# Normalising and turning the second chunk of tokens earlier, by transfers instead of through TensorE

## The chip, the cores and the metric

The kernel runs on one core of a Trainium2 chip. The metric is the device time in microseconds of one execution of the whole program. The core's engines are named as the profile names them: PE (TensorE, matmuls; PEld its weight loads), DVE (VectorE), ACT (ScalarE), POOL (GpSimd) and SP (SyncE, which here only issues transfers). PSUM is the memory that PE writes its products into; SBUF is the working memory of all engines.

## The reference

A sequence of 2048 tokens with 640 features goes through one layernorm, and then through attention with 32 heads of 20 features and through an MLP with its own layernorm and 1536 hidden features. Their results are added to the input.

```python
def _A_ref(x, wqkv, wo):                       # 32 heads, Dh = 20
    qkv = (x @ wqkv).reshape(B, S, 3, H, Dh) ...
    scores = einsum("bhqd,bhkd->bhqk", q, k) * (Dh ** -0.5)
    o = einsum("bhqk,bhkd->bhqd", softmax(scores), v)
    return o.reshape(B, S, D) @ wo
def _B_ref(x, w1, b1, w2, b2):
    h = gelu(_layernorm(x) @ w1 + b1)
    return h @ w2 + b2
x  = A_x                                       # 1 x 2048 x 640, float32
xn = _layernorm(x)
return x + _A_ref(xn, A_wqkv, A_wo) + _B_ref(xn, B_w1, B_b1, B_w2, B_b2)
```

## The kernel before

All matmuls take 16-bit operands in two parts, a high and a low one: `a*b` is computed as high*high + high*low + low*high (the three entries of `PASS`). So each operand is first scaled to a power of two, then copied to float16 on ACT (the high part), and the rest is subtracted on DVE (the low part).

The program has a first part, up to about 227 us, that normalises the tokens and makes Q, K and V, and a long second part in which attention and the MLP run interleaved. The change is in the first part. There the order of each engine's instructions is the order in which the code issues them (`manual_schedule`); nothing is reordered by a planner. An engine does its instructions in that order and waits at the first whose data is not there. SP issues its transfers in the same way. Each transfer of SP's queue also counts on one of eight semaphores in turn, and waits for the transfer eight places ahead of it.

The tokens come in four chunks of 512, loaded as four rows of 128 tokens (`xts[c][j]`, `load_x`). For each chunk c:

- `norm_a(c)` takes mean and variance of the rows on DVE and a power on POOL; `norm_b(c)` makes the row factor exact, normalises the four rows in place (L258) and starts the second layernorm's factor (`norm_b2`, again with a power on POOL); `norm_c(c)` ends that factor on DVE and POOL sends it to DRAM (`rscr`, L274: 512 values of 4 bytes), from where the MLP reads it much later.
- The chunk is turned, so that features lie on the partitions: `xnts[c]`, in a high and a low part. Before, this happens in two ways. The first and second chunk go through PE: `transp` issues 128x128 transposes against an identity into PSUM, `transp_out` evicts them as the high part (ACT) and the low part (DVE). The third and fourth chunk go by `turn(c, j)`: ACT and DVE split row j into its high and low part in a `row` buffer (three of these), and a transposing transfer on SP puts it into `xnts[c]`. In both ways a copy of the finished `xnts[c]` goes to DRAM (`xscr`) for the MLP.
- Five steps tt of `qk(c, tt)` make Q and K of the chunk: each is 30 matmuls into a PSUM buffer of the pool `psS` (three buffers, tag "s"), emptied by `qk_out` (L340 on ACT, L341 on DVE), which also sends both parts to DRAM (`qkscr`). Four calls of `vproj(c, j)` make V from the same turned chunk, emptied by `vproj_out` (L408 on ACT, L410 on DVE).

Into this are fitted the preparations of the weights. In the first chunk: `sums`, `scale_of` and `split_qkv` for K and V (V in the fourth step, tt = 3: L431 on ACT, L432 on DVE); `ask(n)`, which has SP issue the next n loads of w2 (six blocks, L500) and w1 (five blocks, L503); and `some(n)`, the next n slices of squares and splits of w2, w1 and wo, which wait for those loads on ACT.

Before the change, the second chunk's statistics are taken in the third step of the first chunk (tt = 2). `norm_b(1)` comes behind the first V product, `norm_c(1)` behind the second. The transposes of the second chunk stand behind the second and the third V product, in PE's queue between the V products. The second chunk's copy to `xscr` is issued when the last part is evicted; three of the five w1 blocks stand ahead of it in SP's queue, two behind it, and then the third chunk's rows (`load_x(2)`).

Of the kernel before, what the change touches and what calls it, by code (L numbers as in the profile page):

```python
# [18 lines left out]
P = 128  # L19
S, D, H, DH, F = 2048, 640, 32, 20, 1536  # L20
KD = D // P
# [23 lines left out]
def mha_mlp_kernel(tc, x, wqkv, wo, w1, b1, w2, b2, out):  # L45
    nc = tc.nc
# [3 lines left out]
    with (  # L50
# [10 lines left out]
        xscr = dram.tile([P, KD, 2, S], F16, name="xscr")  # L61
# [17 lines left out]
        ident = keep.tile([P, P], F32, name="ident")  # L79
# [84 lines left out]
        with tc.tile_pool(name="pa", bufs=2) as pa, tc.tile_pool(name="pa1", bufs=1) as pa1, tc.manual_schedule():  # L164
# [7 lines left out]
            xts = {}  # L172
# [98 lines left out]
            def norm_c(c):  # L271
                mv, ve, r, r2 = rs.pop(c)
                newton(r2, ve, "b")
                nc.gpsimd.dma_start(rscr[c * 512 : (c + 1) * 512].rearrange("(j p) -> p j", p=P), r2)  # L274

            xnts = {}

            def transp(c, k0, pts):
                if k0 == 0:
                    xnts[c] = pa.tile([P, KD, 2, 512], F16, tag="xnt", name=f"xnt{c}")  # L280
                if k0 + 2 > KD:
                    pt = psM.tile([P, 512], F32, tag="m", name="pt4")[:, None, :]
                else:
                    pt = psS.tile([P, 2, 512], F32, tag="s", name="pt")
                for j in range(4):
                    for k in range(min(2, KD - k0)):
                        nc.tensor.transpose(pt[:, k, j * P : (j + 1) * P],
                                            xts[c][j][:, (k0 + k) * P : (k0 + k + 1) * P], ident)
                pts.append((c, k0, pt))

            def transp_out(c, k0, pt):
                nk = min(2, KD - k0)
                ks = slice(k0, k0 + nk)
                nc.scalar.activation(xnts[c][:, ks, 0, :], pt[:, :nk], AF.Copy)
                nc.vector.tensor_sub(xnts[c][:, ks, 1, :], pt[:, :nk], xnts[c][:, ks, 0, :])
                if k0 + 2 > KD:
                    nc.sync.dma_start(xscr[:, :, :, c * 512 : (c + 1) * 512], xnts[c])
                    del xts[c]

            def turn(c, j):  # L300

                if j == 0:
                    xnts[c] = pa.tile([P, KD, 2, 512], F16, tag="xnt", name=f"xnt{c}")
                xv = xts[c][j].rearrange("p (k n) -> p k n", k=KD)
                row = pa.tile([P, KD, 2, P], F16, tag="row", name="row", bufs=3)
                nc.scalar.activation(row[:, :, 0, :], xv, AF.Copy)
                nc.vector.tensor_sub(row[:, :, 1, :], xv, row[:, :, 0, :])
                nc.sync.dma_start(xnts[c].rearrange("p k s t -> p (k s) t")[:, :, j * P : (j + 1) * P],
                                  row.rearrange("p k s n -> p (k s n)"), transpose=True)
                if j == 3:  # L310
                    nc.sync.dma_start(xscr[:, :, :, c * 512 : (c + 1) * 512], xnts[c])
                    del xts[c]
# [104 lines left out]
            def sums(tag, ws):  # L417
                accs[tag] = squares(ws, junk)

            def scale_of(tag):  # L420
                pw[tag] = pow2(accs[tag], tag)
                scales[tag] = keep.tile([P, 1], F32, name=f"s_{tag}")
                nc.vector.tensor_scalar(scales[tag], pw[tag][1], 4096.0, None, ALU.mult)
                if tag in "qk":
                    q = "qk".index(tag)
                    nc.vector.tensor_scalar(qks[:, q : q + 1], pw[tag][0], QKTOP, 2.0**-22, ALU.min, ALU.mult)

            def split_qkv(n, ks=range(KD), c0=0, c1=D):
                q = "qkv".index(n)
                for k in ks:  # L430
                    nc.scalar.activation(wv[:, k, q, 0, c0:c1], stage[n][:, k, c0:c1], AF.Copy, scale=scales[n])  # L431
                    nc.vector.scalar_tensor_tensor(wv[:, k, q, 1, c0:c1], stage[n][:, k, c0:c1], scales[n],  # L432
                                                   wv[:, k, q, 0, c0:c1], ALU.mult, ALU.subtract)
# [75 lines left out]
            def ask(n):  # L509
                for _ in range(n):  # L510
                    next(asked, None)
# [21 lines left out]
            pts = [psS.tile([P, 2, 512], F32, tag="s", name="pt") for _ in range(2)]  # L533
            pt = [pts[0][:, 0], pts[0][:, 1], pts[1][:, 0], pts[1][:, 1]]
# [17 lines left out]
            for c in range(4):  # L552
                nxt = c + 1 if c < 3 else None
                for tt in range(5):
                    if c == 0 and tt == 1:
                        norm_b2(0)
                        norm_c(0)

                        nc.scalar.activation(junk[:, :1], ones[:, :1], AF.Exp)
                        ps = qk(0, 1, lambda: scale_of("k"))  # L560
                        hl = qk_out(0, 0, first)
                        split_qkv("q", c0=4 * P)
                        split_qkv("k")
                    else:
                        ps = qk(c, tt)
                    if tt == 3:
                        lengths(4)

                    if c == 0:
                        if tt == 0:  # L570
                            split_qkv("q", c0=2 * P, c1=4 * P)
                            sums("k", [stage["k"][:, 0:3], stage["k"][:, 3:]])
                            first = ps
                            continue
                        elif tt == 1:
                            qk_sq(0, 0, hl)
                        elif tt == 2:
                            sums("v", [stage["v"][:, 0:3], stage["v"][:, 3:]])
                            norm_a(1)
                        elif tt == 3:  # L580
                            scale_of("v")
                            split_qkv("v")
                    else:

                        step = tt - (c == 1)
                        if nxt and 0 <= step < 3:
                            (norm_a, norm_b, norm_c)[step](nxt)
                            some(1)
                        else:
                            some(2)  # L590
                    qk_out(c, tt, ps)

                    ask((0, 1, 2, 2, 1)[tt] if c == 0 else 0)
                    if nxt and c > 0 and tt >= 2:
                        for j in ((0,), (1, 2), (3,))[tt - 2]:
                            turn(nxt, j)
                    if c == 3 and tt == 2:
                        early = [load_features(mc) for mc in range(2)]
                if c == 1:
                    load_x(3)  # L600
                if c == 3:
                    stack = load_stack(0, 0)
                    for _ in range(6):
                        next(stack)
                for j in range(4):
                    ps = vproj(c, j)
                    if j == (0 if c == 3 else 1):
                        lengths(10)
                    if c == 0:
                        if j < 2:  # L610
                            (norm_b, norm_c)[j](1)

                        pts = []
                        for k in ((), (0,), (2, 4), ())[j]:
                            transp(1, k, pts)
                        for t in pts:
                            transp_out(*t)
                    if j == 0 and c == 3:
                        shifts()
                        for _ in stack:  # L620
                            pass
                    some(2 if c < 3 else 1)
                    vproj_out(c, j, ps)
# [660 lines left out]
```

## Time and profile before

| | |
|---|---|
| median of 3 runs | 1341.68 us (1340.11 to 1343.48) |
| profiled execution, its own time | 1341.9 us |
| its span, first to last instruction | 1340.0 us |
| mean granted clock of PE | 0.999 |
| busy: PE, ACT, DVE | 1328.6, 1130.1, 1055.9 us |
| first chunk's Q, K and V on PE | from 15.3 us |
| second chunk's first Q and K product on PE | 68.5 us |
| third chunk's | 119.6 us |
| fourth chunk's | 169.6 us |

In a timeline row the first number is the start from the beginning of the span, the second the time from the start of the first to the end of the last instruction in the row, then engine, line, operation, what is written and read, and xN for N instructions; in brackets the idle time of the engine ahead of it and what ended it. In a row of the waits the three numbers are the total, the number of times and the longest. In a row of a table by windows there are, behind the window and its length, the busy time and the count of PE, weight loads, DVE, ACT and POOL, then the granted clock of PE, the share of the 16 transfer engines and the GB/s moved. SPq and POOLq are transfers issued by SP and POOL; a row of the transfers has their count, their size and the median time from issue to landing.

### The profile page before, as it was taken

How to read it: one execution, taken by the hardware profiler on the slowest of the kernel's cores; microseconds unless marked ns; L12 is line 12 of the kernel's file. 1: busy time of each engine (PE TensorE's matmuls, PEld its weight loads, DVE VectorE, ACT ScalarE, POOL GpSimd, SP SyncE). 2: the span in 40 equal slices, each digit the busy share in tenths (PEclk: the TensorE clock that was granted, in tenths of full speed). 3: DMA queues.
4: the chain of work that ended last, by engine and by line, in shares of the span. 5: the costliest groups of instructions: out<-in, count | busy, mean ns of one | idle time of the engine just before them, and what ended most of it. 6: DMA issues, size and time to landing. Idle time of an engine off the chain costs nothing.

```text
span 1340.0 us, 29065 instructions
## 1 busy us (share of the span) xinstructions
PE 1328.6 (99%) x11647; PEld 588.6 (44%) x11647; DVE 1055.9 (79%) x1436; ACT 1130.1 (84%) x1306; POOL 37.5 (3%) x85
## 2 busy tenths in 40 slices
PE   9999999999999999999999999999999999999998
PEld 6645546443344433434433344334333444333366
DVE  7766945998779887978897878888887988888732
ACT  7754525999999999999999999999999999999900
POOL 3010000000000000000000000000000000000000
PEclk9999999999999999999999999999999999999999
DMA  9768731111112232122322032313032323334366
GB/s 279 253 197 183 125 128 58 34 53 43 49 52 78 87 83 73 44 69 67 91 76 71 19 103 56 88 56 94 19 83 78 85 64 103 90 113 121 104 208 187
DMA packets 100150, 129.54 MB, mean 97 GB/s; under 512 B 24276, under 2 KB 66328, under 8 KB 100012
## 3 DMA queue, kind: packets, MB, share of 16 engines
q1 hardware_dynamic: 96652, 120.25, 31.5%
q0 software_dynamic: 2912, 6.90, 2.8%
q8 instruction: 92, 1.51, 0.5%
q10 hardware_dynamic: 448, 0.51, 0.1%
q14 instruction: 46, 0.38, 0.1%
HBM read 82.14 MB, written 42.51 MB: 93 GB/s over the span
## 4 chain that ended last, share of the span: by engine, by line
PE 86%; DVE 6%; ACT 4%; issue 2%; DMA 1%; SPq 0%; ACTq 0%; DVEq 0%; POOL 0%; POOLq 0%
PE o L742 28%; PE s L711 18%; PE py L1006 13%; PE pu L976 10%; PE qkp L325 7%; PE z L1089 4%; PE vp L398 3%; DVE low L725 2%; ACT p L713 1%; PE warm L222 1%; ACT wv L431 1%; DMA oa<-opart 0%; DVE u L914 0%; ACT qkhl L340 0%; DVE u L916 0%
## 5 line engine op out<-in xcount | busy, mean ns | idle before, releaser
L713 ACT ACTIVATE p<-s 128x1024 f32<-128x1024 f32 x1024 | 972.8, 1045 | 35.0 <-PE s L711 28.6
L725 DVE TENSOR_TENSOR low<-p 128x1024 f16<-128x1024 f32 x512 | 614.5, 1219 | 144.9 <-ACT p L713 144.2
L742 PE MATMUL o<-p,vfull 128*32 128x512 bf16 (+1 forms) x4096 | 430.0, 493 | 0.0
L711 PE MATMUL s<-qs,ks 61*128 61x512 f16 x2048 | 311.9, 381 | 1.1 <-ACT p L713 1.1
L711 PEld LDWEIGHTS <-ks 61*128 61x128 f16 x2048 | 61.1, 94 | 280.1 <-issue 279.1
L1006 PE MATMUL py<-w2t,hT 128*128 128x320 f16 x1152 | 178.5, 300 | 0.5 <-DVE u L914 0.3
L976 PE MATMUL pu<-xm,w1t 128*128 128x256 f16 x1440 | 178.2, 273 | 0.0
L976 PEld LDWEIGHTS <-w1t 128*128 128x128 f16 x1440 | 131.0, 98 | 64.6 <-issue 51.0
L1006 PEld LDWEIGHTS <-hT 128*128 128x128 f16 x1152 | 102.5, 98 | 88.5 <-issue 54.1
L325 PE MATMUL qkp<-xnt,wv 128*128 128x512 f16 x600 | 131.1, 379 | 1.4 <-DVE vfull L410 0.9
L742 PEld LDWEIGHTS <-vfull 128*32 128x32 f16 x3072 | 59.8, 95 | 139.2 <-issue 108.5
L742 PE MATMUL o<-low,vfull 128*32 128x512 f16 x1024 | 102.9, 378 | 0.4 <-DVE low L725 0.2
L325 PEld LDWEIGHTS <-wv 128*128 128x128 f16 x600 | 58.1, 98 | 71.4 <-DVE vfull L410 1.2
L742 PEld LDWEIGHTS o<-p,vfull 128*32 128x32 f32 x2048 | 62.5, 108 | 52.6
L1089 PE MATMUL z<-w1t,ot 128*128 128x320 f16 x480 | 69.0, 304 | 0.4 <-DVE acc L1047 0.4
L340 ACT ACTIVATE qkhl<-qkp,qks 128x1024 f16<-128x1024 f32 (+1 forms) x24 | 23.2, 967 | 54.6 <-PE qkp L325 33.0
L398 PE MATMUL vp<-wv,xnt 128*128 128x320 f16 x480 | 66.7, 299 | 0.0
L1089 PEld LDWEIGHTS <-ot 128*128 128x128 f16 x480 | 46.7, 99 | 24.3 <-issue 5.9
L398 PEld LDWEIGHTS <-xnt 128*128 128x128 f16 x480 | 46.7, 98 | 18.4
L341 DVE SCALAR_TENSOR_TENSOR qkhl<-qkp,qks,qkhl 128x1024 f16<-128x1024 f32 (+1 forms) x24 | 26.5, 1105 | 32.6 <-ACT qkhl L340 32.5
L1047 DVE SCALAR_TENSOR_TENSOR acc<-z,sc,acc 128x320 f32<-128x320 f32 x32 | 17.4, 546 | 40.7 <-PE z L1089 40.5
L763 ACT ACTIVATE ev<-o 128x512 f32<-128x512 f32 x64 | 39.3, 614 | 2.7 <-PE o L742 2.7
(190 smaller groups left out, 672.4 us busy)
## 6 DMA issues: line engine op xcount, KB each, us to landing
qkscr<-qkhl SPq DMA_DIRECT2D x40, 256.0 KB
opart<-ev SPq DMA_DIRECT2D x124, 80.0 KB
ks<-qkscr SPq DMA_DIRECT2D x120, 80.0 KB
qs<-qkscr SPq DMA_DIRECT2D x192, 40.0 KB
oa<-opart SPq DMA_DIRECT2D x32, 240.0 KB
xt<-in_A_x_dram SPq DMA_DIRECT2D x16, 320.0 KB
xscr<-xnt SPq DMA_DIRECT2D x4, 1280.0 KB
xm<-xscr SPq DMA_DIRECT2D x8, 640.0 KB
```

Of the source, the lines that this page charges most:

```text
L325: nc.tensor.matmul(ps[:, i, :], wv[:, k, q, a, mm * P : (mm + 1) * P], xnts[c][:, k, b, :], start=(k + n == 0), stop=(k == KD - 1 and n == 2))
L340: nc.scalar.activation(hl[:, 0, i0:i1], ps[:, i0:i1], AF.Copy, scale=a)
L341: nc.vector.scalar_tensor_tensor(hl[:, 1, i0:i1], ps[:, i0:i1], a, hl[:, 0, i0:i1], ALU.mult, ALU.subtract)
L398: nc.tensor.matmul(ps[:, hf, :320], xnts[c][:, k, a, j * P : (j + 1) * P], wv[:, k, 2, b, hf * 320 : (hf + 1) * 320], start=(n == 0), stop ...
L711: nc.tensor.matmul(ps[:, a, :], ks[64 * a : 64 * a + 61, kb * P : (kb + 1) * P], qs[64 * a : 64 * a + 61, cc * 512 : (cc + 1) * 512], star ...
L713: nc.scalar.activation(pt, ps, AF.Exp, scale=QS)
L725: nc.vector.tensor_sub(low, pt, upper(pt))
L742: nc.tensor.matmul(pv.o[32 * q : 32 * q + 32, :], src[:, v0 - PAD * (1 - q % 2) :][:, :32], t, start=q not in pv.begun, stop=last, skip_gr ...
L763: nc.scalar.activation(evs[g, hf][:, cc], pv.o, AF.Copy)
L976: nc.tensor.matmul(ps[:, i], w1v[:, k, (f + i) // 4, a, fo_ : fo_ + P], xnt[:, k, b, :], start=(n == 0), stop=(n == 3 * KD - 1))
L1006: nc.tensor.matmul(ps[:, :320], hTs[mc][:, f, a, j * P : (j + 1) * P], w2v[:, f, b, hf * 320 : (hf + 1) * 320], start=(n == 0), stop=(n == ...
L1089: nc.tensor.matmul(ps[:, :320], ot[:, k, a, j * P : (j + 1) * P], wov[:, k, b, h * 320 : (h + 1) * 320], start=(n == 0), stop=(n == 3 * KD ...
```

## The change

The second chunk is turned as the third and the fourth are. `norm_b(1)` goes ahead of the V weights' scale in the fourth step of the first chunk (tt = 3), and `turn(1, 0)` and `turn(1, 1)` between that scale and the V split. `norm_c(1)`, `turn(1, 2)` and `turn(1, 3)` stand at the end of the fifth step (tt = 4). The transposes through PE and their evictions between the V products are gone. `ask` and `some` stay where they were; in SP's queue the four transposing transfers and the copy to `xscr` now stand ahead of all five w1 blocks, since those are asked for behind the V products.

```diff
-            def transp(c, k0, pts):
...
-                        nc.tensor.transpose(pt[:, k, j * P : (j + 1) * P],
-                                            xts[c][j][:, (k0 + k) * P : (k0 + k + 1) * P], ident)
...
-            def transp_out(c, k0, pt):
...
-                nc.scalar.activation(xnts[c][:, ks, 0, :], pt[:, :nk], AF.Copy)
-                nc.vector.tensor_sub(xnts[c][:, ks, 1, :], pt[:, :nk], xnts[c][:, ks, 0, :])
-                if k0 + 2 > KD:
-                    nc.sync.dma_start(xscr[:, :, :, c * 512 : (c + 1) * 512], xnts[c])
-                    del xts[c]
...
                         elif tt == 3:
+                            norm_b(1)
                             scale_of("v")
+                            turn(1, 0)
+                            turn(1, 1)
                             split_qkv("v")
...
                     ask((0, 1, 2, 2, 1)[tt] if c == 0 else 0)
+                    if c == 0 and tt == 4:
+                        norm_c(1)
+                        turn(1, 2)
+                        turn(1, 3)
...
                     ps = vproj(c, j)
                     if j == (0 if c == 3 else 1):
                         lengths(10)
-                    if c == 0:
-                        if j < 2:
-                            (norm_b, norm_c)[j](1)
-
-                        pts = []
-                        for k in ((), (0,), (2, 4), ())[j]:
-                            transp(1, k, pts)
-                        for t in pts:
-                            transp_out(*t)
```

`turn`, which is called and stands unchanged:

```python
            def turn(c, j):
                if j == 0:
                    xnts[c] = pa.tile([P, KD, 2, 512], F16, tag="xnt", name=f"xnt{c}")
                xv = xts[c][j].rearrange("p (k n) -> p k n", k=KD)
                row = pa.tile([P, KD, 2, P], F16, tag="row", name="row", bufs=3)
                nc.scalar.activation(row[:, :, 0, :], xv, AF.Copy)
                nc.vector.tensor_sub(row[:, :, 1, :], xv, row[:, :, 0, :])
                nc.sync.dma_start(xnts[c].rearrange("p k s t -> p (k s) t")[:, :, j * P : (j + 1) * P],
                                  row.rearrange("p k s n -> p (k s n)"), transpose=True)
                if j == 3:
                    nc.sync.dma_start(xscr[:, :, :, c * 512 : (c + 1) * 512], xnts[c])
                    del xts[c]
```

More of the change, by code (lines that the diff above doesn't have):

```diff
@@ L276, in mha_mlp_kernel @@
             xnts = {}
-            def transp(c, k0, pts):
-                if k0 == 0:
-                    xnts[c] = pa.tile([P, KD, 2, 512], F16, tag="xnt", name=f"xnt{c}")
-                if k0 + 2 > KD:
[L282 to L287, printed above, removed]
-                                            xts[c][j][:, (k0 + k) * P : (k0 + k + 1) * P], ident)
-                pts.append((c, k0, pt))
-            def transp_out(c, k0, pt):
-                nk = min(2, KD - k0)
-                ks = slice(k0, k0 + nk)
-                nc.scalar.activation(xnts[c][:, ks, 0, :], pt[:, :nk], AF.Copy)
-                nc.vector.tensor_sub(xnts[c][:, ks, 1, :], pt[:, :nk], xnts[c][:, ks, 0, :])
-                if k0 + 2 > KD:
-                    nc.sync.dma_start(xscr[:, :, :, c * 512 : (c + 1) * 512], xnts[c])
-                    del xts[c]
             def turn(c, j):
```

## The prediction

> **What bounds the kernel now.** I read the page first: engine times, then the waits of TensorE (PE) over the first 240 us, then the timelines of PE, VectorE (DVE), ScalarE (ACT), GpSimd (POOL) and the transfer queue (SP) from 40 to 165 us, and last the transfers and the windows.
>
> ```profile
> PE 1328.6 (99%) x11647; PEld 588.6 (44%) x11647; DVE 1055.9 (79%) x1436; ACT 1130.1 (84%) x1306; POOL 37.5 (3%) x85
> ```
> ```profile
> PE qkp L325 <- DVE vfull L410: 0.9, 1, 0.9
> ```
>
> PE is busy for 1328.6 of 1340.0 us, so a microsecond put on its path, or taken off it, arrives at the end, unless another chain is late. The second row is the longest wait of PE between its start and 240 us: 0.9 us just before the third chunk's first Q and K product, which starts at 119.6. There another chain, not PE, sets the time already. So two things have to be followed: PE's own queue up to the second chunk (it reaches it at 68.5 us), and the chain that feeds the third.
>
> **What leaves PE.** The stretch in question, PE's timeline:
>
> ```profile
> 57.65 1.09 PE L287 MATMUL pt<-ident,xt 128*128 128x128 f32 x8
> 58.58 4.24 PE L398 MATMUL vp<-wv,xnt 128*128 128x320 f16 x30
> 62.65 1.47 PE L287 MATMUL pt<-ident,xt 128*128 128x128 f32 x12
> 63.96 4.24 PE L398 MATMUL vp<-wv,xnt 128*128 128x320 f16 x30
> 68.04 0.28 PE L113 MATMUL mxp<-acc,ones 128*128 128x6 f32 x2
> 68.52 26.06 PE L325 MATMUL qkp<-xnt,wv 128*128 128x512 f16 x120 [0.20 <-ACT vfull L408]
> ```
>
> The 20 transposes hold the next product up from 57.65 to 58.58 and from 62.65 to 63.96: 0.93 + 1.31 = 2.24 us, all on PE's path. With them go three evictions on ACT and three subtractions on DVE; four row copies and four subtractions come instead, about the same work.
>
> **What moves ahead of the V weights.** DVE's timeline, then one row of the later chunk's turn:
>
> ```profile
> 42.38 0.16 DVE L114 TENSOR_REDUCE lo_v<-mxp 128x1 f32<-128x2 f32 x1
> ...
> 44.37 4.07 DVE L432 SCALAR_TENSOR_TENSOR wv<-w1t,s_v,wv 128x640 f16<-128x640 f32 x5 [0.90 <-ACT wv L431]
> 48.36 1.28 DVE L341 SCALAR_TENSOR_TENSOR qkhl<-qkp,qks,qkhl 128x1024 f16<-128x1024 f32 x1
> 50.34 1.28 DVE L341 SCALAR_TENSOR_TENSOR qkhl<-qkp,qks,qkhl 128x1024 f16<-128x1024 f32 x1 [0.71 <-ACT qkhl L340]
> 51.54 0.15 DVE L228 TENSOR_TENSOR at<-r 128x4 f32<-128x4 f32 x1
> ...
> 54.81 0.17 DVE L268 TENSOR_SCALAR ve<-ve 128x4 f32<-128x4 f32 x1
> ```
> ```profile
> 98.13 1.55 DVE L307 TENSOR_TENSOR row<-xt,row 128x640 f16<-128x640 f32 x2
> ```
>
> `norm_b(1)` is the stretch from 51.54 to 54.98, 3.44 us, and now stands before the V scale, so that scale starts at 45.8 instead of 42.38, and the ACT half of the V split 3.4 us later. DVE then has its six small scale steps (42.38 to 43.47, 1.1 us) and the two subtractions (1.55) before its half of the split, which runs from 48.5 to 52.5 (five steps, 4.07 us) instead of ending at 48.4. The V products take 4.1 us each (58.58 to 62.65), so the first of the two that end ahead of 57.65 begins at 49. It takes its five weight blocks about as fast as DVE now makes them, so it loses next to nothing. Behind the split the fourth step's subtraction (L341, 1.28 us) ends at 53.8 instead of 49.6, and it frees the PSUM buffer of the second V product, which PE reaches at 53.1: a wait of 0.7 us. PE is then ready for the second chunk at 68.52 - 2.24 + 0.7 = 67.0, a gain of 1.5 us, if the turned rows are there.
>
> The fifth step's subtraction ends at 55.1, `norm_c(1)`'s four small steps (as from 51.54, 0.8 us in all) at 55.9, the last two row subtractions at 56.7 and 57.5. So POOL sends the second chunk's 2 KB of row factors (rscr) at about 56.2, and SP issues the turning transfers 0 and 1 at about 48 and 49, transfers 2 and 3 from about 57 on, behind the fourth and fifth steps' Q and K writes and three blocks of w2.
>
> **When the turned rows land.** Here the forecast turns. SP's timeline at the fourth chunk, POOL's factors of the third and fourth chunk, and the traffic around the last of them (the column before GB/s is the DMA share):
>
> ```profile
> 148.92 1.36 SPq L308 DMA_TRANSPOSE xnt<-row  x1
> 150.38 2.21 SPq L346 DMA_DIRECT2D qkscr<-qkhl  x2
> 153.54 5.42 SPq L308 DMA_TRANSPOSE xnt<-row  x2
> 159.06 1.05 SPq L346 DMA_DIRECT2D qkscr<-qkhl  x2
> 160.48 1.60 SPq L308 DMA_TRANSPOSE xnt<-row  x1
> 164.95 0.54 SPq L311 DMA_DIRECT2D xscr<-xnt  x1
> ```
> ```profile
> 95.24 0.79 POOL L274 DMA_DIRECT2D rscr<-r  x1 [3.41 <-DVE r L231]
> ...
> 144.38 0.81 POOL L274 DMA_DIRECT2D rscr<-r  x1 [2.75 <-DVE r L231]
> ```
> ```profile
> rscr<-r POOLq DMA_DIRECT2D x4, 2.0 KB, 11.9
> ```
> ```profile
> 74.00:80.00 6.00, 6.00 (x30) 2.70 (x29) 1.88 (x2) 2.45 (x2) 0.00 (x0) 1.00 1.02 405
> 146.00:149.00 3.00, 3.00 (x17) 1.34 (x16) 2.25 (x5) 2.95 (x5) 0.00 (x0) 1.00 0.55 151
> 149.00:155.00 6.00, 6.00 (x37) 3.51 (x36) 5.90 (x10) 3.06 (x5) 0.00 (x0) 1.00 1.38 18
> 155.00:161.00 6.00, 6.00 (x60) 4.21 (x61) 5.43 (x15) 3.58 (x5) 0.00 (x0) 1.00 1.20 282
> ```
> ```profile
> 108.08 0.74 ACT L306 ACTIVATE row<-xt 128x640 f16<-128x640 f32 x1 [5.15 <-issue]
> ```
>
> A turning transfer by itself is short: the last one is issued at 160.48, and the write that waits for all four goes out at 164.95, 4.5 us later. On that row transfers 2 and 3, issued from 57 on, would land at about 65, in time for 67.0.
>
> [...]
>
> But the factors of 2 KB take 11.9 us to land, and late in that time the whole queue nearly stands: after those sent at 144.38 the traffic falls to 18 GB/s from 149 to 155, and is back at 282 behind it. The same at the third chunk: its factors go out at 95.24, and the ACT row at 108.08, which reuses the buffer of that chunk's first turned row, waits until 108, that is 12.8 us behind them. In the changed kernel the factors go out at 56.2, so the queue stands from about 61 to 68.1, and transfers 2 and 3 fall into it with one w2 block (640 KB, 1.6 us at the 405 GB/s of the first window) ahead of them. Behind the standstill I add 3.5 us for that block and the two transfers; the bounds are 2 us (block nearly through) and 5.4 us (two issues took that on SP at 153.54). They land at 71.6 (70 to 73.5), and PE waits from 67.0 until then, 3.1 us later than before.
>
> **What stands behind them on SP.** The second chunk's copy to xscr waits for all four transfers, and SP issues in order; behind it now stand all five w1 blocks (three of them went out ahead of it before) and the third chunk's x rows:
>
> ```profile
> 53.44 1.94 SPq L503 DMA_DIRECT2D w1t<-in_B_w_dram  x3
> 66.63 0.54 SPq L297 DMA_DIRECT2D xscr<-xnt  x1
> 67.21 2.04 SPq L503 DMA_DIRECT2D w1t<-in_B_w_dram  x2
> 69.35 2.82 SPq L181 DMA_DIRECT2D xt<-in_A_x_dram  x4
> ```
> ```profile
> 81.26 0.89 DVE L243 BATCH_NORM_STATS2 st<-xt 128x6 f32<-128x320 f32 x2 [3.04 <-DMA xt<-in_A_x_dram]
> ```
> ```profile
> wos<-in_A_wo_dram POOLq DMA_DIRECT2D x5, 320.0 KB, 3.8
> ```
>
> The third chunk's statistics wait for those x rows until 81.26 already, and DVE then works through `norm_a`, `norm_b`, the turn and `norm_c` almost without a gap up to the factors at 95.24; these hold the ACT row until 108.08, and from there ACT, POOL's wo loads and DVE run to the 0.9 us wait at 119.6. So the chain that decides at 119.6 starts with the x rows. After the change, behind an issue at 71.7 (sizes by the tensors' shapes): xscr 1280 KB, five blocks of 768 KB and the first x of 320 KB are 5.57 MB, 13.8 us at 405 GB/s; beyond its bytes (0.8 us) a load of 320 KB needed 3.0 us. The first x rows land at 88.5, 7.2 us later than 81.26. PE meanwhile is only 3 to 5 us late (the fifth step's buffer also waits for the shifted DVE chain), so the chain sets the third chunk's start, at 119.6 + 7.2. From there to the attention the order is that of before, and I carry the 7.2 us to the end.
>
> **Sum.** The profiled execution took 1341.9 us (span 1340.0), 0.2 above the median of 1341.68. -2.2 (transposes), +0.7 (second V product), +4.6 (landing) give +3.1 on PE at the second chunk; the chain's +7.2 covers that at the third: 1341.9 + 7.2 = 1349.1, or 1349 against the median. With the landing's bounds (70 to 73.5) it is +5.6 to +9.1.
>
> **Rivals.**
> In time (not slower by what can be measured; about 0.3%, 4 us, can be told from no change): the second chunk's factors do not hold the transfers up. For it: transfers run in 4.5 us undisturbed. Against: the standstill behind the factors at 144.38 and the 12.8 us behind those at 95.24. Then transfers land at 65 to 66.5, PE gains up to 1.5 us at the second chunk, and the x rows, still behind three more w1 blocks, come at 65.5 + 16.8 = 82.3 at the earliest, +1, or +4 if the factors then slow the copy and the loads instead: 1342.5 to 1346. It decides if the landing is before 68.4, where the chain's shift is 4 us.
>
> Faster: were everything hidden, the change could win 2.24 us of transposes and the 0.9 us wait, 3.1 in all, under the 4 us; nothing in these rows gives more. 1338.6.
>
> The clock:
>
> ```profile
> 1284.80:1288.20 3.40, 3.40 (x15) 1.96 (x14) 0.00 (x0) 0.00 (x0) 0.00 (x0) 0.50 0.70 196
> ```
>
> Near the end, behind a pause of PE, the granted clock is 0.50 for 3.4 us. My forecast has PE idle for 4.6 us before the second chunk and for 2 to 4 before the third. Half the clock for 3.4 us costs 1.7; the first is covered by the chain, the second is not: 1350.8. Against: one pause among few is all that the trace shows. [...]
>
> Heavier: the standstill catches the w2 blocks and writes too, and transfers 2 and 3 land at 75 to 76: +11, 1353.
>
> That the change does not do what it says is excluded: the program's queues stand as told.
>
> **Chances.** Forecast 0.42, clock 0.20, heavier 0.14, in time 0.21, faster beyond 0.3% 0.03. Slower by over 0.3%: 0.42 + 0.20 + 0.14 + 0.03 of the in-time case's upper end = 0.79; same 0.18; faster 0.03. Likeliest 1349; the range takes in the heavier case and most of the in-time one, 1343 to 1353.5.
>
> **What would show it.** In the profile after: no pt rows from L287; PE's second-chunk product starting near 71.6 behind a wait on a transfer; the three V-split rows 3.4 to 4.2 us later; POOL's factors near 56; traffic under 50 GB/s somewhere from 60 to 68; x rows' statistics near 88; PE's wait before the third chunk grown to 2 to 4 us. I am wrong if the second chunk starts before 68, or if the statistics start by 83.

## Result and profile after

The changed kernel takes 1349.39 us (median of 6 runs, 1347.11 to 1350.72) where the kernel before took 1342.03 us on the same chip (6 runs, 1340.11 to 1343.75): a ratio of 1.0060, with a 95% interval of 1.0048 to 1.0071. The change makes the kernel slower by some 7 to 8 us. The profiled execution of the changed kernel took 1350.72 us, with a span of 1348.8 us. Lines behind line 298 of the file stand 22 lower than before: the Q and K product is L303 (was L325), its eviction L318 and L319, the turn L284 to L286, the copy to xscr L289, the V product L376, the squares of w2 and w1 L442 and L450.

First the page's busy times, then PE's timeline from the V products to the third chunk (start, length, engine, line, operation, tiles, shape, count, and in brackets the idle time ahead with what ended it):

```profile
PE 1332.3 (99%) x11627; PEld 589.5 (44%) x11627; DVE 1054.7 (78%) x1437; ACT 1129.8 (84%) x1307; POOL 37.5 (3%) x85
```
```profile
59.33 8.32 PE L376 MATMUL vp<-wv,xnt 128*128 128x320 f16 x60
71.42 0.60 PE L113 MATMUL mxp<-acc,ones 128*128 128x6 f32 x2 [3.77 <-ACT junk L442]
72.30 28.98 PE L303 MATMUL qkp<-xnt,wv 128*128 128x512 f16 x120 [0.28 <-DMA xnt<-row]
...
102.50 6.65 PE L303 MATMUL qkp<-xnt,wv 128*128 128x512 f16 x30 [0.56 <-DVE qkhl L319]
...
125.98 4.26 PE L303 MATMUL qkp<-xnt,wv 128*128 128x512 f16 x19
```

The pt rows are gone. The second chunk's first product starts at 72.30 where it started at 68.52, and its 120 matmuls take 28.98 us where they took 26.06. The third chunk starts at 125.98, 6.4 us later than 119.59, and no wait stands ahead of it any more; before there was one of 0.9 us. A new wait of 0.86 us ahead of the third chunk's V products (159.94) makes 7.4 of the 6.4, and from there on the shift stays at about 7.0 to 7.4 us up to the end of the attention.

Next the windows of the same stretch (busy time and count of PE, PEld, DVE, ACT and POOL, then the granted clock, the DMA share and GB/s), and the rows of POOL, SP and ACT that go with them:

```profile
60.00:62.00 2.00, 2.00 (x17) 1.45 (x15) 0.57 (x3) 1.97 (x5) 0.00 (x0) 1.00 1.08 377
62.00:68.00 6.00, 5.65 (x42) 3.84 (x40) 0.83 (x1) 1.80 (x3) 0.00 (x0) 1.00 1.30 80
...
71.42:78.25 6.83, 6.55 (x17) 2.58 (x18) 0.93 (x6) 0.54 (x1) 0.00 (x0) 0.50 0.75 217
```
```profile
56.02 0.79 POOL L274 DMA_DIRECT2D rscr<-r  x1 [9.03 <-DVE r L231]
```
```profile
56.36 0.52 SPq L478 DMA_DIRECT2D w2t<-in_B_w_dram  x1
56.98 13.12 SPq L286 DMA_TRANSPOSE xnt<-row  x2
72.22 0.56 SPq L289 DMA_DIRECT2D xscr<-xnt  x1
72.82 4.60 SPq L481 DMA_DIRECT2D w1t<-in_B_w_dram  x5
```
```profile
70.01 1.27 ACT L442 ACTIVATE junk<-w2t 128x1280 bf16<-128x1280 f32 x1 [6.21 <-DMA w2t<-in_B_w_dram]
...
81.05 1.48 ACT L450 ACTIVATE junk<-w1t 128x1536 bf16<-128x1536 f32 x1 [9.09 <-DMA w1t<-in_B_w_dram]
...
110.25 0.72 ACT L284 ACTIVATE row<-xt 128x640 f16<-128x640 f32 x1
```
```profile
90.74 0.89 DVE L243 BATCH_NORM_STATS2 st<-xt 128x6 f32<-128x320 f32 x2 [1.45 <-DMA xt<-in_A_x_dram]
```

Six microseconds behind the factors' issue at 56.02 the traffic falls from 377 to 80 GB/s. Two things stand in it together: the two turning transfers, and the last block of w2, which ScalarE needs for the sum of squares that PE takes in (mxp) ahead of the second chunk. The share of the 16 transfer engines stays at 1.30 in this window: they are taken, but little moves. PE waits 3.77 us for that sum and then 0.28 for the turned rows, so both are late by about the same amount. Behind the pause the granted clock is 0.50 for 6.83 us. The copy goes out at 72.22, the first w1 block is squared at 81.05 (before at 68.37), and the third chunk's statistics start at 90.74 (before at 81.26).

### The profile page after: what moved, and what is told of

It is laid out like the page before. It is cut to its first block, busy times and chain, and to the rows that moved or that the text cites. A ratio compares the mean times of both kernels' runs of the same rounds, so it can differ in the third digit from the quotient of the medians.

```text
span 1348.8 us, 29033 instructions
## 1 busy us (share of the span) xinstructions
PE 1332.3 (99%) x11627; PEld 589.5 (44%) x11627; DVE 1054.7 (78%) x1437; ACT 1129.8 (84%) x1307; POOL 37.5 (3%) x85
## 4 chain that ended last, share of the span: by engine, by line
PE 79%; DVE 8%; DMA 6%; ACT 3%; issue 2%; SPq 1%; ACTq 0%; POOL 0%; DVEq 0%; POOLq 0%
PE o L718 28%; PE s L687 18%; PE py L982 12%; PE pu L952 10%; PE z L1065 4%; PE vp L376 2%; PE qkp L303 2%; DVE low L701 2%; DMA wos<-in_A_wo_dram 2%; ACT p L689 1%; DMA xt<-in_A_x_dram 1%; DVE qkhl L319 1%; PE warm L222 1%; DMA xnt<-row 1%; DVE st L243 1%
## 5 line engine op out<-in xcount | busy, mean ns | idle before, releaser
L303 PE MATMUL qkp<-xnt,wv 128*128 128x512 f16 x600 | 134.0, 385 | 1.0 <-DVE qkhl L319 0.6
L303 PEld LDWEIGHTS <-wv 128*128 128x128 f16 x600 | 58.7, 99 | 73.0 <-issue 4.3
L376 PE MATMUL vp<-wv,xnt 128*128 128x320 f16 x480 | 67.2, 299 | 1.7 <-DVE qkhl L319 0.9
L318 ACT ACTIVATE qkhl<-qkp,qks 128x1024 f16<-128x1024 f32 (+1 forms) x24 | 23.1, 964 | 50.4 <-PE qkp L303 24.8
L319 DVE SCALAR_TENSOR_TENSOR qkhl<-qkp,qks,qkhl 128x1024 f16<-128x1024 f32 (+1 forms) x24 | 26.5, 1104 | 38.9 <-ACT qkhl L318 38.8
L376 PEld LDWEIGHTS <-xnt 128*128 128x128 f16 x480 | 46.7, 98 | 21.0 <-issue 2.6
```

The costliest lines, as they stand in the source:

```text
L303: nc.tensor.matmul(ps[:, i, :], wv[:, k, q, a, mm * P : (mm + 1) * P], xnts[c][:, k, b, :], start=(k + n == 0), stop=(k == KD - 1 and n == 2))
L318: nc.scalar.activation(hl[:, 0, i0:i1], ps[:, i0:i1], AF.Copy, scale=a)
L319: nc.vector.scalar_tensor_tensor(hl[:, 1, i0:i1], ps[:, i0:i1], a, hl[:, 0, i0:i1], ALU.mult, ALU.subtract)
L376: nc.tensor.matmul(ps[:, hf, :320], xnts[c][:, k, a, j * P : (j + 1) * P], wv[:, k, 2, b, hf * 320 : (hf + 1) * 320], start=(n == 0), stop ...
```

## The experiments

Two causes are in question. **A**: the factors' standstill, PE's pause by it, and the half clock behind the pause. **B**: the chain that the prediction let decide, with the copy, all five w1 blocks and the third chunk's x rows behind the turning transfers. **C** is the rival that turning transfers are dear by themselves. The table sums up what follows. "Third" is the start of the third chunk's first product in the profiled execution against 119.59; ratios are to the kernel before on the same chips, since medians of different chips differ by 1 to 2 us. "Third" and "second" count from the span's start, and the first Q and K product itself starts at 15.34 us before, at 15.81 in the changed kernel and between 15.06 and 16.04 in the other runs, which no edit here touches: counted from it, the changed kernel's third chunk is 5.9 us late. Half a microsecond between two rows is therefore not read as a difference of the edits.

| kernel | second chunk starts | third, us later | median, us | ratio (95%) |
|---|---|---|---|---|
| before | 68.52 | 0 | 1342.03 | 1 |
| changed | 72.30 | 6.4 | 1349.39 | 1.0060 (1.0048 to 1.0071) |
| factors_late | 67.69 | 6.7 | 1352.46 | 1.0083 (1.0064 to 1.0102) |
| early_transposes | 71.58 | 4.2 | 1347.85 | 1.0043 (1.0028 to 1.0058) |
| x_first | 72.65 | 12.5 | 1355.54 | 1.0100 (1.0085 to 1.0115) |
| warm_pause | 73.36 | 11.5 | 1353.30 | 1.0084 (1.0069 to 1.0099) |
| copy_last | 72.90 | 6.0 | 1348.98 | 1.0044 (1.0030 to 1.0059) |
| late_copy_last | 67.86 | 4.1 | 1347.19 | 1.0021 (1.0000 to 1.0042) |
| sp_factors | 72.21 | 8.1 | 1348.66 | 1.0044 (1.0029 to 1.0059) |
| short_factors | 71.73 | 2.3 | 1346.41 | 1.0026 (1.0012 to 1.0040) |
| short_copy_last | 72.73 | 3.3 | 1346.65 | 1.0020 (1.0008 to 1.0031) |
| after_rows_j3 | 67.13 | 2.2 | 1346.37 | 1.0009 (0.9994 to 1.0024) |
| before_rows_j3 | 68.47 | -1.0 | 1340.81 | 0.9983 (0.9968 to 0.9998) |
| all_moved | 68.71 | -0.7 | 1344.14 | 1.0004 (0.9992 to 1.0016) |

**The factors sent later** (factors_late).

```diff
 if c == 0 and tt == 4:
-    norm_c(1)
     turn(1, 2)
...
 (norm_a, norm_b, norm_c)[step](nxt)
+if c == 1 and step == 0:
+    norm_c(1)
```

> The changed kernel, but POOL sends the second chunk's 2 KB of row factors behind the third chunk's statistics (about 80 us) and not at 56. Theory A (the factors' standstill from 62 to 68 holds up the last w2 block and the turned rows 2 and 3; PE idles 3.8 us and then runs 6.8 us at half clock): the two turning transfers land at 63 to 66, the second chunk starts at 67 to 68, at full clock, and the time is 1341 to 1344 us, with up to 2 us more if the factors hold something else up later. Theory B (the SP queue's order: the x rows behind the copy and five w1 blocks set the third chunk): x rows land some 6 us earlier than in the changed kernel but still near 83 to 84: 1343 to 1346. Theory C (the turning transfers are slow by themselves, and SP stands while it issues them): the second chunk still starts near 72, 1348 to 1350.

The second chunk starts where theory A put it, at full clock, and theory C falls: without the factors the same transfers are in time (ScalarE squares the last w2 block at 65.42, in the changed kernel at 70.01). But the kernel is no faster than the changed one, where theory A had it 5 to 8 us faster. PE's timeline, the window behind its pause, and DVE's first eviction of the second chunk:

```profile
67.69 26.06 PE L303 MATMUL qkp<-xnt,wv 128*128 128x512 f16 x120
...
98.38 9.01 PE L303 MATMUL qkp<-xnt,wv 128*128 128x512 f16 x30 [3.98 <-DVE qkhl L319]
...
126.31 26.07 PE L303 MATMUL qkp<-xnt,wv 128*128 128x512 f16 x120 [1.39 <-DVE vfull L388]
```
```profile
96.40:103.20 6.80, 4.83 (x12) 1.79 (x13) 3.90 (x14) 1.31 (x2) 2.19 (x3) 0.50 0.34 47
```
```profile
84.06 1.28 DVE L319 SCALAR_TENSOR_TENSOR qkhl<-qkp,qks,qkhl 128x1024 f16<-128x1024 f32 x1 [15.09 <-ACT qkhl L318]
```

A new wait of 3.98 us stands ahead of the second chunk's last Q and K product, for a buffer that the evictions free late, with half the clock behind it, and one of 1.39 ahead of the third chunk. ScalarE squared the first w1 block at 76.3, still 8 us later than before, its evictions stand behind that square, and DVE idled 15.09 us for them; the statistics then stand between the evictions. The factors, sent at 91.28, made their standstill behind 96 (47 GB/s) and held a write for which ScalarE's eviction at 103.53 waited 5.37 us. So with PE's own delay taken away, the chain behind the copy and the standstill at its new place gave a shift of 6.7.

**The standstill with the transposes kept** (early_transposes): the kernel before, its normalisation and factors as early as in the changed kernel.

```diff
 elif tt == 3:
+    norm_b(1)
     scale_of("v")
...
+if c == 0 and tt == 4:
+    norm_c(1)
...
-    if j < 2:
-        (norm_b, norm_c)[j](1)
```

> The kernel before, with its transposes on TensorE, but the second chunk's normalisation in the fourth step and its factors sent behind the fifth, as in the changed kernel. Theory A: the factors' standstill alone makes the last w2 block land near 69, ScalarE squares it near 70, and PE waits for that sum until 70 to 72, two to three us behind the kernel before, with the half clock behind the pause: 1345 to 1349 us. Theory C (turning transfers are the cost): no turning transfer in this stretch, so 1341.5 to 1343.5. Theory B: the copy goes out at 66 and three w1 blocks ahead of it as before, so 1341.5 to 1343.5.

```profile
62.00:68.00 6.00, 6.00 (x49) 4.71 (x47) 2.65 (x3) 4.53 (x7) 0.00 (x0) 1.00 1.11 103
```
```profile
70.98 0.39 PE L113 MATMUL mxp<-acc,ones 128*128 128x6 f32 x2 [2.06 <-ACT junk L464]
71.58 27.75 PE L325 MATMUL qkp<-xnt,wv 128*128 128x512 f16 x120 [0.20 <-ACT vfull L408]
```

With no turning transfer in the stretch, the traffic falls to 103 GB/s all the same, PE waits 2.06 us for the w2 sum, and the second chunk takes 27.75 us instead of 26.06. That is 4.2 us at the third chunk, 0.7 of it from the V products, which end later behind the normalisation. Moving the factors ahead is the larger part of the loss, and the turned rows have no part in these 4.2.

**The x rows first** (x_first), a test of theory B:

```diff
 turn(1, 3)
+load_x(2)
...
-if c == 0:
-    load_x(2)
```

> The changed kernel with the third chunk's x rows issued ahead of the five w1 blocks. Theory A: the second chunk starts at 72.3 at half clock as in the changed kernel, the statistics come 8 to 13 us earlier (78 to 83), and nothing is won, since PE sets the third chunk's start: 1348 to 1350.5 us. Theory B (the x rows' chain carries the loss): 1342 to 1345.

Both theories missed: it lost another 6 us, and the statistics came later, at 94.40. ScalarE's and PE's rows:

```profile
84.68 1.48 ACT L450 ACTIVATE junk<-w1t 128x1536 bf16<-128x1536 f32 x1 [12.36 <-DMA w1t<-in_B_w_dram]
```
```profile
106.10 9.12 PE L303 MATMUL qkp<-xnt,wv 128*128 128x512 f16 x30 [4.61 <-DVE qkhl L319]
```

So here the head of the chain is not the x rows but the first w1 block: its square stands on ScalarE ahead of the second chunk's evictions, and the evictions' DVE half stands ahead of the statistics. Whatever holds w1 back holds everything behind it.

**PE kept busy in the pause** (warm_pause):

```diff
 ps = vproj(c, j)
+if j == 3 and c == 0:
+    warm(13)
```

> The changed kernel with 13 matmuls of ones (3.6 us, no part of the result) in PE's pause ahead of the second chunk. Theory A: the second chunk starts at 72.3 as in the changed kernel, but at full clock: 2 to 3 us less, 1346 to 1347.5. Theory B (the chain sets the third chunk, and the half clock is covered by it): no change, 1348.5 to 1350.

```profile
72.48:79.30 6.82, 6.33 (x30) 3.04 (x31) 0.93 (x6) 0.53 (x1) 0.00 (x0) 1.00 0.75 214
```
```profile
73.36 26.06 PE L303 MATMUL qkp<-xnt,wv 128*128 128x512 f16 x120 [0.49 <-DMA xnt<-row]
...
103.03 8.11 PE L303 MATMUL qkp<-xnt,wv 128*128 128x512 f16 x30 [2.97 <-DVE qkhl L319]
...
131.07 26.07 PE L303 MATMUL qkp<-xnt,wv 128*128 128x512 f16 x120 [2.93 <-DVE vfull L388]
```
```profile
118.19 0.74 ACT L284 ACTIVATE row<-xt 128x640 f16<-128x640 f32 x1 [5.85 <-DMA xnt<-row]
```

PE's pause is down to 1.71 us, and the half clock is gone, 26.06 us as before: here it had come with the long pause. The product and the copy were 1 us later than in the changed kernel, and the 2.9 us that the full clock won came back as a wait of 2.97 ahead of the last Q and K product, as theory B says: the half clock taken away alone wins nothing. What neither theory had, and why the time lies above both ranges, is the 2.93 us ahead of the third chunk. It comes from the third chunk's own factors: here the first turned row was issued at 104.37 and the factors at 105.27, the row fell into their standstill, and ScalarE waited 5.85 us for its buffer. In the changed kernel the row went out at 103.84, had landed at 106.85, and that wait is missing (the row at 110.25 above). In all three kernels SP begins to issue the row ahead of POOL's factors; the order in which the two issues end differs. SP is through with the row at 105.21 and POOL with the factors at 105.53 in the changed kernel, but at 106.36 and 106.06 here, and at 96.24 and 96.03 in the kernel before, which waits too. The same holds in early_transposes (the row's issue ends behind the factors', and ScalarE waits 4.72 us) and in x_first, copy_last and late_copy_last (it ends ahead, and there is no wait). So some 0.3 us decided; no edit tested it by itself.

**The copy last** (copy_last): the changed kernel, only the copy moved.

```diff
 if j == 3:
-    nc.sync.dma_start(xscr[:, :, :, c * 512 : (c + 1) * 512], xnts[c])
+    if c > 1:
+        nc.sync.dma_start(xscr[:, :, :, c * 512 : (c + 1) * 512], xnts[c])
...
 load_x(2)
+nc.sync.dma_start(xscr[:, :, :, 512:1024], xnts[1])
```

> The changed kernel with its factors as they are, and only the second chunk's copy moved behind the w1 blocks and x rows. If PE itself is late (standstill and half clock) and the chain behind the copy only comes beside it: the second chunk still starts at 72 to 72.5 at half clock, the w1 squares and statistics come 5 to 8 us earlier than in the changed kernel (first square near 74, statistics near 83 to 85), the wait ahead of the second chunk's last Q and K product (0.6 us) goes, and the third chunk is 4.5 to 6 us later than in the kernel before against 6.4: 1346.5 to 1349 us. If the chain sets the third chunk, as the prediction had it: 1 to 2 us later than before, 1342 to 1344.5.

```profile
72.90 28.77 PE L304 MATMUL qkp<-xnt,wv 128*128 128x512 f16 x120 [0.29 <-DMA xnt<-row]
...
102.18 6.64 PE L304 MATMUL qkp<-xnt,wv 128*128 128x512 f16 x30
...
125.64 26.06 PE L304 MATMUL qkp<-xnt,wv 128*128 128x512 f16 x120
```

The first w1 square came at 75.58 and the statistics at 85.23, 5.5 us earlier each, and the third chunk moved by 0.3 (PE's second chunk began 0.6 later here). In the changed kernel the chain behind the copy costs next to nothing, because PE itself is as late: with the chain out of the way, only the 0.56 us ahead of the last Q and K product goes. **Both moved** (late_copy_last: this edit and the factors sent later) shows the other side:

> The changed kernel with both suspected causes moved: factors sent behind the third chunk's statistics, and the second chunk's copy (1280 KB) issued behind the w1 blocks and the third chunk's x rows instead of ahead of them. Theory A+B (PE's pause by the standstill and the chain through ScalarE's w1 squares and the x rows each cost about 6.5 us at the third chunk, and cover one another): second chunk at 67.7, the first w1 block lands near 72 and not 76, statistics near 81 to 83, third chunk 119 to 123: 1341 to 1346. If only A were right, late factors would have been enough; if the w1 blocks and x rows aren't the head of the chain, 1350 to 1353 as with late factors alone.

The second chunk at 67.86, the first w1 square at 70.43, the statistics at 78.67, and the third chunk at +4.1, better than with either move alone, though the time is above the 1341 to 1346 of theory A+B. Most of the rest is a wait of 3.95 us ahead of the last Q and K product with half the clock behind it (8.34 us for 6.63), and here it is the standstill: the factors went out at 85.23, and ScalarE's eviction waited 11.91 us for the landing of an earlier write:

```profile
95.49 0.69 ACT L319 ACTIVATE qkhl<-qkp,qks 128x512 f16<-128x512 f32 x1 [11.91 <-DMA qkscr<-qkhl]
```

To see the chain without any standstill, the factors' many writes themselves had to go.

**What makes the standstill.** The same 512 writes of 4 bytes from SP in place of POOL (sp_factors, `nc.gpsimd` to `nc.sync` in `norm_c`):

> The changed kernel with the factors' 512 writes of 4 bytes sent by SP in place of POOL, for all four chunks. If the many small writes make the standstill, in whichever queue: traffic falls under 100 GB/s for some 6 us behind each of them as before, 1347 to 1353 us. If POOL's queue makes it: no low stretch, second chunk at 67 to 69, 1339 to 1345.

and 4 rows of 512 bytes from POOL (short_factors), by a small transposing matmul:

```diff
-nc.gpsimd.dma_start(rscr[c * 512 : (c + 1) * 512].rearrange("(j p) -> p j", p=P), r2)
...
+nc.tensor.transpose(pt[:4, :P], r2, ident)
...
+nc.vector.tensor_copy(rt, pt[:4, :P])
+nc.gpsimd.dma_start(rscr[c * 512 : (c + 1) * 512].rearrange("(j p) -> j p", p=P), rt)
```

> The changed kernel, but each chunk's factors are first transposed by one small matmul (128x4 to 4x128) and go out from POOL, behind the first V product, as 4 rows of 512 bytes instead of 512 elements of 4 bytes. Theory A (the many small writes make the standstill): the factors land within 4 us, traffic never falls under 150 GB/s between 60 and 68 while loads are queued, the second chunk starts at 67 to 69 at full clock. The first w1 block still lands behind the copy, some 6 us later than in the kernel before, and the statistics come near 84 to 86, but the third chunk's factors no longer hold the turned rows for 5 us: third chunk at 118 to 122, 1339 to 1344 us. If the standstill belongs to POOL's queue and not to the number of writes: second chunk at 72, 1347 to 1351.

The windows, first from SP, then as rows (short_factors, and after_rows_j3, which follows below), and the issue's row of short_factors (KB each, median us to landing; in the kernel before 11.9):

```profile
68.00:72.00 4.00, 0.09 (x1) 0.00 (x1) 0.93 (x6) 0.25 (x1) 0.00 (x0) 0.98 0.65 38
```
```profile
62.00:68.00 6.00, 4.96 (x54) 3.60 (x54) 2.14 (x5) 2.72 (x5) 0.53 (x1) 1.00 0.72 154
```
```profile
68.00:72.00 4.00, 4.00 (x20) 1.85 (x19) 0.51 (x4) 0.00 (x0) 0.99 (x2) 1.00 1.00 297
```
```profile
rscr<-rt POOLq DMA_DIRECT2D x4, 2.0 KB, 3.4
```

It is the many small writes, not POOL's queue: from SP they only hold the traffic up later, since they were issued 1.5 us later. Part of the 38 GB/s is a queue that has run short, since the last w2 block was through by then; the turned rows were not, and PE waits 4.12 us for them. As rows the factors land in 3.4 us, and the low stretch is gone: the 154 GB/s are the mean of a busy stretch up to 66 and of two microseconds behind it in which nothing is left to move. The edit also sends them later, at 63.28 and not at 56.02. So the clearer row is that of after_rows_j3: two chunks' factors go out at 67.89 with the copy and the w1 blocks queued, and the traffic from 68 to 72 is 297 GB/s. The kernel of short_factors lost 4.3 us of PE to the new copies (waits of 2.45 and 1.84 us on them in the V stage), so its second chunk is still at 71.73, and the next one with the copy last as well (short_copy_last) has the same fault:

> The changed kernel with the short factors (4 rows of 512 bytes) and the second chunk's copy behind the w1 blocks and x rows. Theory A+B: no standstill, no half clock, second chunk at 67 to 68, statistics at 79 to 82, no 0.9 us wait ahead of the third chunk at 118 to 119.5: 1338 to 1342 us, about 1 to 3 under the kernel before. If something else bounds the third chunk: 1343 or more.

That run tells nothing apart at the third chunk: PE's own waits for the copies, and half the clock behind one of them (5.91 us for a V row of 4.24), set it at +3.3. With the transposing matmul behind the last V product, in a bank that is free there, these waits go (after_rows_j3; before_rows_j3 is the same edit in the kernel before):

> The changed kernel with the short factors (4 rows of 512 bytes per chunk) as before, but transposed behind the last V product in a bank that is free there, so that PE does not wait for the copies (it waited 4.3 us for them in the first try). Theory A+B: second chunk at 67 to 68.5 at full clock; the first w1 block still lands behind the copy near 76, so PE waits 0 to 4 us ahead of the second chunk's last Q and K product and the third chunk starts at 119 to 122.5: 1341 to 1345 us. If the chain behind the copy costs nothing without a standstill: 1338.5 to 1341.

> The kernel before, its transposes on TensorE, with the same short factors: what the change is worth when no standstill is there on either side is read against the run above. Second chunk at 68.5 as in the kernel before; the third chunk's turned rows no longer wait 5 us behind its factors, so PE's 0.9 us wait goes: 1340 to 1342.5 us. If the standstills cost the kernel before more than that wait (qk_out's buffers, the fourth chunk): 1338 to 1340.

PE's rows of the changed kernel with row-wise factors, then of the kernel before with them:

```profile
67.13 26.06 PE L320 MATMUL qkp<-xnt,wv 128*128 128x512 f16 x120
...
96.50 8.34 PE L320 MATMUL qkp<-xnt,wv 128*128 128x512 f16 x30 [2.66 <-DVE qkhl L336]
```
```profile
118.62 26.06 PE L342 MATMUL qkp<-xnt,wv 128*128 128x512 f16 x120
```

Without standstills the change wins 1.4 us at the second chunk (67.13; 1.2 counted from the first product) and loses it again to the chain behind the copy: 2.66 us of waiting and 3.4 us at half clock. That is theory B by itself, +2.2 at the third chunk. The kernel before with rows loses its 0.9 us wait. Of the two, the second came out in the forecast time, and the first 1.4 us above it.

**All moved** (all_moved): row-wise factors, the copy last, and the normalisation and first two turns behind the fourth step's eviction.

```diff
 elif tt == 3:
-    norm_b(1)
     scale_of("v")
-    turn(1, 0)
-    turn(1, 1)
     split_qkv("v")
...
 qk_out(c, tt, ps)
+if c == 0 and tt == 3:
+    norm_b(1)
+    turn(1, 0)
+    turn(1, 1)
```

> The changed kernel with the short factors, the second chunk's copy behind the w1 blocks and x rows, and the normalisation and first two turned rows behind the fourth step's eviction, so that the V weights' split is not put off. Theory A+B: V products begin at 48.5 to 49.5 without the four waits for the split (0.8 us) and the 0.9 us for the buffer, second chunk at 65.8 to 68 if the turned rows are there by then (they are issued some 5 us later), no half clock, third chunk at 116.5 to 119: 1337 to 1341 us, 1 to 5 under the kernel before. If the turned rows land late even without a standstill: second chunk at 69 to 71 and 1341 to 1344.

PE's rows, behind one of before_rows_j3:

```profile
67.99 0.38 PE L285 MATMUL rp<-ident,r 128*4 128x128 f32 x2
```
```profile
65.81 0.38 PE L285 MATMUL rp<-ident,r 128*4 128x128 f32 x2
67.90 0.39 PE L113 MATMUL mxp<-acc,ones 128*128 128x6 f32 x2 [1.71 <-ACT junk L460]
68.71 26.06 PE L321 MATMUL qkp<-xnt,wv 128*128 128x512 f16 x120 [0.42 <-ACT vfull L404]
```

PE is through with the V products at 65.81, 2.2 us earlier than in before_rows_j3, and 1.8 us earlier counted from the first Q and K product (15.19 and 15.57): most of the price of the transposes is won. Then it waits 1.71 us for the squares of w2's last block and 0.42 for an eviction, and starts the second chunk 0.2 us later than the kernel before. At the third chunk the two kernels are about level (-0.7 and -1.0), and the forecast of 1337 to 1341 missed. So even in the best form tried here the change brings nothing, since the w2 sum has to be there ahead of the second chunk and comes no earlier. The fastest kernel is the one before with row-wise factors: 0.9983 (0.9968 to 0.9998).

## Why the prediction was right, and where it was not

The forecast of 1349 stands against 1349.39. The sign and the first cause are shown: the factors' standstill moved into the turning transfers' way. The way from there to the third chunk was not the forecast one, and that the number came out this close is in part luck. Step by step:

- **The transposes, 2.24 us.** About right as a size: all_moved shows PE 1.8 to 2.2 us earlier. It is never kept.
- **The V weights.** Forecast: the first V product loses next to nothing, the second 0.7 us. Measured: four waits, 0.8 us together, and 0.9 us. A term mis-sized by 1 us. PE was through with the V products at 67.65; the forecast's 67.0 for the second chunk, less the 0.48 us from the sum's matmul on (68.04 to 68.52), put that at 66.5. Of the difference 0.5 us is the later start of the first product.
- **The factors and the landing.** Forecast 56.2 and a landing at 71.6; measured 56.02, and the second chunk at 72.30. The traffic fell as forecast. The step has the last w2 block in the same hole, but only as bytes ahead of the turned rows. What it left out is that PE needs that block's sum ahead of the second chunk (ScalarE waited 6.21 us for the block), so that PE would have waited even with the transposes kept; early_transposes shows that.
- **The half clock at the second chunk.** The prediction gave it 3.4 us, priced it at 1.7 and put it down as "covered by the chain". It lasted 6.83 us and cost PE 2.9 (28.98 for 26.06). Covered it was, but at another place than meant, and narrowly: with it, PE reached the second chunk's last Q and K product only 0.56 us ahead of the chain, and without it (warm_pause) PE waited 2.97 us there instead.
- **The chain sets the third chunk, +7.2.** This step failed. The x rows did come late, by 9.5 us and not 7.2, and beside them the first w1 block, whose square holds the second chunk's evictions and which the prediction did not name. But the chain no longer ended in a wait ahead of the third chunk: the first turned row got out ahead of the factors by some 0.3 us, so that ScalarE's 5.15 us wait of before was gone. The chain met PE ahead of the second chunk's last Q and K product and held it there for 0.56 us; all else is PE's own delay: +3.8 (second chunk), +2.9 (half clock), +0.7 (0.6 before the last Q and K product, and small gaps), -0.9 (the wait that went) and -0.1 of smaller differences are the 6.4 measured. copy_last shows it: the chain 5.5 us earlier, the third chunk only 0.3. The 7.4 that reached the attention took one more wait, the 0.86 us at the third chunk's V products, which the forecast does not have.
- **Why the number still came out.** With PE's delay taken away, the chain with the standstill at its new place gives 6.7 (factors_late). The two bounds are almost equal and lie beside each other, so naming the wrong one cost little; that they are almost equal is luck. The clock rival had a half clock that came, but at the other pause than the one it priced.

The tail adds a difference that lies outside the change's stretch: in the profiled execution of the changed kernel the half clock near the end lasted 6.8 us (from 1290), in that of before 3.4.

## What to carry to other kernels

Before moving a step earlier, list its small transfers as well as its arithmetic: 2 KB in 512 writes of 4 bytes held up the transfers queued with it for some 6 us, and put where PE needed them it was the larger part of this loss. Turn such a result into a few long rows first (4 rows of 512 bytes landed in a median of 3.4 us here, the 512 writes in 11 to 12), behind work where its copies make no engine wait. Time taken off the bounding engine is kept only if the next thing that it takes in comes earlier too; here the sum of w2's squares did not (PE waited 1.71 us for it in all_moved). And when two chains are late by about the same time, taking one away shows nothing: move both, one at a time and together.

## What the runs showed of the hardware

- 512 writes of 4 bytes held up the traffic from either queue: 80 GB/s for 6 us behind POOL's (the changed kernel), 38 GB/s for 4 us behind SP's (sp_factors), the latter with little else queued. The same 2 KB as 4 rows of 512 bytes from POOL landed in a median of 3.4 us (short_factors) instead of 11 to 12. In after_rows_j3 the median is 4.3 us, and 297 GB/s went on moving from 68 to 72 us, beside two of them sent at 67.89.
- Behind some pauses of PE the granted clock was 0.50, behind others 1.00, and the length of the pause alone does not settle which. It was 0.50 for 6.83 us behind 3.77 us in the changed kernel, for 6.80 us (from 96.40) behind 3.98 us in factors_late and for 3.40 us (from 102.60) behind 2.97 us in warm_pause, where the 120 matmuls behind 2.93 us took 26.07 us, as at full clock. Near the program's end it was 0.50 for 3.41 us behind a pause of 1.60 us in the kernel before, and for 6.83 us behind one of 1.38 us in the changed kernel.
- The products' times tell the same. Behind 2.45 us a V row of 30 matmuls took 5.91 us in short_copy_last and 4.24 us in short_factors. The last Q and K product took 8.34 us instead of 6.63 behind 3.95 us (late_copy_last), 2.66 us (after_rows_j3) and 2.08 us (sp_factors): 1.71 us more, which is about 3.4 us of half clock, an estimate from these times.
- In the changed kernel the half clock begins at 71.42 and at 1289.98 us, in the kernel before at 1284.80 and, behind PE's last matmul, at 1339.42: 1218.56 and 54.62 us apart, 357.0 and 16.0 times the 3.413 us that it lasts from 1284.80. What settles whether it comes behind a pause, and for how long, is not shown.
- SP was held while it issued turning transfers: two of them took 13.12 us at 56.98 in the changed kernel, with 309 GB/s moving from 57 to 61.7 and 106 from 61.75 to 70.1, and 8.21 us at 57.23 in factors_late, without the factors, but 2.91 us at 47.67 in the changed kernel, with 209 GB/s moving from 47.6 to 50.6 and ahead of the next loads.
